# The experts' weights of a fused attention and mixture kernel: their transfers issued from GpSimd's queue instead of SyncE's

## The chip, the cores and the metric

The kernel runs on one core of one Trainium2 chip. The metric is the device time of one execution in microseconds (us); the median of three runs of the kernel before is 1012.65 us (1012.44 to 1013.64). In the rows PE is TensorE's matmul stream and PEld its weight loads, DVE is VectorE, ACT is ScalarE, POOL is GpSimd, SP is SyncE (SPq: instructions that SP's sequencer runs, here the issuing of DMAs).

## The reference

Three stages follow one another. First, attention inside chunks of 64 positions (8 batches, 8 heads, 576 positions, 64 numbers a head). Its output, 4608 tokens of 512 numbers, goes through a wide layer with a squared ReLU. Then comes a soft mixture of 8 experts with 4 slots each:

```python
x = attn(q, k, v)                                  # (4608, 512)
h = np.maximum(x @ w_in, 0.0)                      # w_in (512, 2048)
x = h * h @ w_out                                  # w_out (2048, 512)
logits = x @ phi                                   # phi (512, 32)
d = softmax(logits, axis=0)                        # over the tokens
slot_input = (d.T @ x).reshape(8, 4, 512)
for e in range(8):
    slot_out[e] = np.maximum(slot_input[e] @ w1[e], 0.0) @ w2[e]   # w1[e] (512, 1024), w2[e] (1024, 512)
out = softmax(logits, axis=1) @ slot_out           # (4608, 512), float32
```

No slot input is complete before the last token has gone through the wide layer, so the experts' matmuls stand at the end. Their weights, 32 MB in w1 and w2, are wanted only there.

## The kernel before

**Tiles and blocks.** The tokens are cut into 36 tiles of 128 (two chunks of 64 for all heads), and the tiles into 13 blocks of 1, 2 and then 3 tiles. For each of 16 slices f of the wide layer a step computes `hps = wi[f] x xb` (L764, 12 matmuls of 128x384), ReLU and square on ACT, a split into two halves of a number, `gh` (ACT, L178) and `gl` (DVE, L807), and adds `gh x wo[f]` and `gl x wo[f]` to the block's three output banks (L825, L826 with `gh`; L827 with `gl`). Numbers are carried as pairs of parts, so each product costs three matmuls. While PE works on block b, the other engines run the attention of the tiles of block b+1; POOL has four operations of it, the halves of v (L433), the normalised weights (L484) and their low part (L497). Two DMA transposes of a tile go through SP (L444, L500).

**After a block.** The generator `soft` turns a finished block into logits and running sums: `largest_of`, then for blocks 5 to 11 each tile's two parts are written to `x16` (ACT L1019, DVE L1020), transposed by a DMA from SP into `x2T` (L1024, three of them), and multiplied with phi (L1032, 36 matmuls for three tiles j = 0, 1, 2). The last block takes another way (L1044, L1056), and it is followed by the chain that joins the running maxima and sums, on whose way POOL has six operations: low parts of the transposed routing weights (`cT`, L1270) and copies for the next ones (`c`, L187), which PE transposes (L1256).

**The experts' weights.** `units` lists 64 pieces of 512 KB: 32 of w1 (128 rows of 1024 numbers, 4 KB in a row) and 32 of w2 (four runs of 256 numbers, 1 KB each, in a partition). There is no room for them during the kernel, so `load_units` puts a piece wherever a buffer has had its last reader: `give(...)` hands a buffer over, `load_units` takes the next piece of the list, and issues it whole or, where the two free halves do not lie side by side, in two halves of 256 KB. The first six go out in block 4 (`parts_of_wo` gives the second half of `wo`), most others when the attention's buffers of the last two tiles, 34 and 35, come free, and then one by one in the last block, as each `wi` and `wo` has been used for the last time. The rest follow in the experts' stage itself, with the output stores behind them.

**What sets the order.** Up to block 2 a list written by the kernel's own planner fixes every engine's order. From there on the Tile framework's scheduler orders each engine's queue by its own estimates, PE excepted after the end of the last block, where the program's order holds. Each queue is worked off in order: an instruction that waits holds up all behind it, a DMA's issue as well. All DMAs before were issued by SP: attention's loads (L377), w_in and w_out (L271), the transposes, the experts' pieces (L1194, L1197 for w1, L1203, L1208 for w2), the output.

Of the kernel before, what the change touches and what calls it, by code (L numbers as in the profile page):

```python
# [74 lines left out]
def kernel(  # L75
# [25 lines left out]
    dve, act, pool, pe, sp = nc.vector, nc.scalar, nc.gpsimd, nc.tensor, nc.sync  # L101
# [654 lines left out]
    def moe_h(b, f):  # L756
        n = blocks[b][1] * P
        xb = xb_b[max(group[b], 1) % 2][:, :, :, bank0.get(b, 0) * P :]
        bank = ps_h.tile([P, 512], F32, tag="h", name="hps")
        hp = bank[:, :n]  # L760
        nm = 0
        for kt in range(KT):
            for wl, xl in ((0, 0), (0, 1), (1, 0)):
                pe.matmul(  # L764
                    hp, wi[f][:, wl, kt], xb[:, xl, kt, :n], start=(nm == 0), stop=(nm == 3 * KT - 1)
                )
                nm += 1
        gt[b, f] = {"hp": hp, "n": n}
        while after_h:
            after_h.pop(0)(bank)  # L770
# [12 lines left out]
    def moe_relu(b, f, eng="act"):  # L783
        r = gt[b, f]
        r["g"] = half_of("g", F32)[:, : r["n"]]
        sc = (act_w if parts16(b) else inv_w)[:, f : f + 1]
        if eng == "act":
            act.activation(out=r["g"], in_=r["hp"], func=ACTF.Relu, scale=sc)  # L788
        else:
            dve.tensor_scalar(r["g"], r["hp"], sc, 0.0, ALU.mult, ALU.max)  # L790

    def moe_square(b, f, eng="act"):
        g = gt[b, f]["g"]
        if eng == "act":
            act.activation(out=g, in_=g, func=ACTF.Square)  # L795
        else:
            (dve if eng == "dve" else pool).tensor_tensor(out=g, in0=g, in1=g, op=ALU.mult)

    def moe_gh(b, f, eng="act"):
        r = gt[b, f]  # L800
        r["gh"] = half_of("gh", F16 if parts16(b) else F32R)[:, : r["n"]]
        copy(eng, r["gh"], r["g"])

    def moe_gl(b, f, eng="dve"):
        r = gt[b, f]
        r["gl"] = half_of("gl", F16 if parts16(b) else F32R)[:, : r["n"]]
        (dve if eng == "dve" else pool).tensor_tensor(  # L807
            out=r["gl"], in0=r["g"], in1=r["gh"] if parts16(b) else r["gh"].bitcast(F32),
            op=ALU.subtract,
        )  # L810
# [365 lines left out]
    home, free, size_of = {}, [], {}  # L1176
    todo = list(units)

    def load_units():
        while todo and len(free) > 1:  # L1180

            whole = [x for x in range(len(free) - 1) if free[x][0] is free[x + 1][0]]
            x = whole[0] if whole else 0
            a, b = free[x : x + 2]
            del free[x : x + 2]
            u = todo.pop(0)
            m, ch, e, kk = u
            whole_home = a[0] is b[0] and a[1] + 512 == b[1]
            places = [t[:, o : o + 512] for t, o, _ in (a, b)]
            home[u] = (a, b)  # L1190
            if m == 0:
                src = w1[e, kk * P : (kk + 1) * P, :]
                if whole_home:
                    sp.dma_start(out=a[0][:, a[1] : a[1] + 1024], in_=src)  # L1194
                else:
                    for h, pl in enumerate(places):
                        sp.dma_start(out=pl, in_=src[:, h * 512 : (h + 1) * 512])  # L1197
            else:
                src = w2[e, kk * RT * P : (kk + 1) * RT * P, ch * DH : (ch + 1) * DH].rearrange(
                    "(t p) d -> p t d", p=P  # L1200
                )
                if whole_home:
                    sp.dma_start(  # L1203
                        out=a[0][:, a[1] : a[1] + 1024].rearrange("p (t d) -> p t d", d=DH), in_=src
                    )
                else:
                    for h, pl in enumerate(places):
                        sp.dma_start(  # L1208
                            out=pl.rearrange("p (t d) -> p t d", d=DH), in_=src[:, h * RT // 2 : (h + 1) * RT // 2]
                        )  # L1210

# [74 lines left out]
    def run_gen(t, gen):  # L1286
        def go(t=t):
            try:
                next(gen)
            except StopIteration:  # L1290
                return
            at(t + 1, lambda: go(t + 1))
        at(t, lambda: go(t))
# [245 lines left out]
    def put_until(t):  # L1539
        while tokens and tokens[0][0] < t:  # L1540
            put(*tokens.pop(0)[2:])
# [4 lines left out]
    def give(*tags):  # L1546
        for pl, tag, n in tags:
            if tag in kept_tags[: (C_CHAIN + 1) // 2]:
                empty.update({(tag, 0), (tag, 512)})
            else:  # L1550
                freed(pl, tag, n)
        load_units()
# [8 lines left out]
    pl = (NT - 1) % 2  # L1561
# [12 lines left out]
    while t < end or any(x >= t for x in slots):  # L1574
        put_until(t + 1)
        b, f = steps[t] if 0 <= t < len(steps) else (None, None)
        if b is not None:
            moe_h(b, f)
            moe_relu(b, f)
            moe_square(b, f)  # L1580
            if (b, f) == (NB - 1, NF - 1):
                give((big, f"xb{b % 2}", 1536))
        for fn in slots.pop(t, []):
            fn()
        if b is not None:
            moe_gh(b, f)
            moe_gl(b, f)
            if b == NB - 1 and f % 2:
                give((big, f"wi{f // 2}", 1024))
        if 0 <= t - LAG < len(steps):  # L1590
            b, f = steps[t - LAG]
            moe_out(b, f, f == 0, f == NF - 1)
            if b == F16_FROM - 1:
                parts_of_wo(f)
            if b == NB - 1 and f == 0:
                give((big, "wo16", 512))
            elif b == NB - 1 and (f % 2 == 0 or f == NF - 1):
                give((big, f"wo{(f - 1) // 2}", 1024))
            if f == NF - 1:
                if b == NB - 1:  # L1600
                    if TAIL_ORDER:
                        ctx.enter_context(
                            tc.manual_schedule(
                                engines={getattr(mybir.EngineType, e) for e in TAIL_ORDER}
                            )
                        )
                    give(*[(big, x, 512) for x in ("g0", "g1", "gh", "gl")])
                moe_store(b, True)
                gen = soft(b)
                run_gen(t + 1 if b < NB - 1 else t, gen)  # L1610
                if b == NB - 1:
                    slots[t].pop()()
        t += 1
# [221 lines left out]
```

## Time and profile before

| | us |
|---|---|
| median of three runs | 1012.65 |
| profiled execution | 1012.46 |
| its span on the core | 1010.7 |
| PE busy | 942.7 |
| DVE busy | 659.5 |
| ACT busy | 545.1 |
| POOL busy | 263.6 |

The span is the time from the first to the last instruction; the profiled execution took 1.76 us more than its span. Busy times overlap. PE's idle time lies mostly in the first fifth and in the last tenth of the span; in between it has work nearly all the time, and the other engines wait for it or for one another.

The experts' pieces are 92 issues on SP in all, 36 of 512 KB and 56 of 256 KB.

### The profile page before, as it was taken

To read this page: it belongs to the slowest core of one execution; us is meant where nothing else is said; L and a number is where in the kernel's file an instruction comes from. 1 tells how busy PE (TensorE), PEld (TensorE's weight loads), DVE (VectorE), ACT (ScalarE), POOL (GpSimd) and SP (SyncE) were. 2 spreads that over 40 slices of the span, in tenths; PEclk is the share of its full clock that TensorE was granted. 3 is DMA by queue.
4 is the path that set the end of the run, shared out by engine and by line. 5 is a ranking of instruction groups with operands and counts; after the bars stand their busy time and mean duration, and the time that the engine had idled before them with its cause. 6 is when DMAs were issued, how large, how long until landed. Compare 5 with 4: busy or idle time off the path is not lost.

```text
span 1010.7 us, 18866 instructions
## 1 busy us (share of the span) xinstructions
PE 942.7 (93%) x7277; PEld 569.5 (56%) x7277; DVE 659.5 (65%) x1395; ACT 545.1 (54%) x1022; POOL 263.6 (26%) x265
## 2 busy tenths in 40 slices
PE   6778999899999999999999999999999999999892
PEld 5566666577666665555555555555555545555352
DVE  4998958656788877677677686586686742322242
ACT  4677664445567664455555564555555644544232
POOL 3587544423124441121112111111211110000200
PEclk9799999999999999999999999999999999999997
DMA  6767232325432463334354454353353651466898
GB/s 161 228 175 194 74 122 53 64 63 88 97 68 63 108 143 64 63 69 90 63 98 82 67 117 78 63 95 64 63 95 63 143 139 53 105 198 191 275 359 258
DMA packets 270762, 117.70 MB, mean 116 GB/s; under 512 B 230224, under 2 KB 264016, under 8 KB 270672
## 3 DMA queue, kind: packets, MB, share of 16 engines
q1 hardware_dynamic: 270672, 116.49, 48.1%
q8 instruction: 57, 0.93, 0.4%
q14 instruction: 33, 0.27, 0.1%
HBM read 78.71 MB, written 9.44 MB: 87 GB/s over the span
## 4 chain that ended last, share of the span: by engine, by line
PE 64%; DVE 17%; DMA 6%; ACT 3%; issue 3%; SPq 3%; POOL 2%; DVEq 0%; POOLq 0%; ACTq 0%
PE hps L764 25%; PE x L825 9%; PE x L827 9%; PE x L826 9%; DMA qkv<-in_k_dram 3%; DVE qk L293 2%; DVE stage L298 2%; PE ehps L1657 2%; PE sop L1773 2%; DVE gl L807 1%; SPq L377 1%; DVE qk L292 1%; PE misc L1147 1%; DMA qkT<-qk 1%; DMA x2T<-x 1%
## 5 line engine op out<-in xcount | busy, mean ns | idle before, releaser
L764 PE MATMUL hps<-xb,wi 128*128 128x384 f16 (+2 forms) x2412 | 411.3, 320 | 3.1 <-DVE wi L331 2.3
L764 PEld LDWEIGHTS <-wi 128*128 128x128 f16 x2412 | 224.5, 98 | 156.2 <-issue 14.3
L825 PE MATMUL x<-wo,gh 128*128 128x512 f16 (+1 forms) x576 | 229.4, 398 | 2.9 <-DVE x2sb L891 2.9
L826 PE MATMUL x<-wo,gh 128*128 128x512 f16 (+1 forms) x576 | 222.1, 386 | 0.0
L827 PE MATMUL x<-wo,gl 128*128 128x512 f16 (+1 forms) x576 | 206.6, 389 | 7.7 <-DVE gl L807 4.5
L807 DVE TENSOR_TENSOR gl<-g,gh 128x384 f16<-128x384 f32 (+1 forms) x162 | 94.8, 590 | 96.8 <-ACT gh L178 95.4
L788 ACT ACTIVATE g<-hps,act_w 128x384 f32<-128x384 f32 x128 | 73.9, 577 | 154.3 <-PE hps L764 136.7
L178 ACT ACTIVATE gh<-g 128x384 f16<-128x384 f32 (+3 forms) x196 | 99.8, 509 | 20.7 <-PE x L826 16.4
L484 POOL TENSOR_TENSOR ex<-ex,rs 128x512 f32<-128x512 f32 x29 | 31.2, 1077 | 287.0 <-DVE rs L481 127.2
L795 ACT ACTIVATE g<-g 128x384 f32<-128x384 f32 (+2 forms) x196 | 99.7, 509 | 5.1
L172 DVE TENSOR_REDUCE am<-qkv 128x1 bf16<-128x512 f32 x94 | 63.7, 685 | 47.5 <-DMA qkv<-in_k_dram 23.8
L433 POOL TENSOR_SCALAR vbd<-qkv,as 64x512 f16<-64x512 f32 x58 | 53.8, 927 | 155.9 <-DVE ai L208 144.9
L827 PEld LDWEIGHTS <-gl 128*128 128x128 f16 x384 | 37.1, 98 | 47.4 <-DVE gl L807 4.6
L825 PEld LDWEIGHTS <-gh 128*128 128x128 f16 x384 | 37.6, 98 | 42.6 <-ACT g L788 5.0
L788 ACT ACTIVATE g<-hps,inv_w 128x384 f32<-128x384 f32 (+1 forms) x72 | 38.6, 536 | 40.5 <-PE hps L764 26.3
L826 PEld LDWEIGHTS <-gh 128*128 128x128 f16 x384 | 37.6, 98 | 39.3 <-issue 4.0
L423 DVE SCALAR_TENSOR_TENSOR qk<-qkv,as,qk 128x512 f16<-128x512 f32 x58 | 55.0, 958 | 0.9 <-ACT qk L418 0.5
L448 DVE COPY qbd<-qkT 64x1024 f16<-64x1024 f16 x58 | 26.6, 459 | 44.2 <-DMA qkT<-qk 43.7
L438 DVE SCALAR_TENSOR_TENSOR vbd<-qkv,as,vbd 64x512 f16<-64x512 f32 x58 | 51.3, 884 | 3.8 <-POOL vbd L433 2.8
L807 POOL TENSOR_TENSOR gl<-g,gh 128x384 fp32r<-128x384 f32 (+2 forms) x39 | 43.1, 1108 | 36.8 <-ACT gh L178 28.4
L474 ACT ACTIVATE ex<-ex,es 128x512 f32<-128x512 f32 x29 | 20.8, 718 | 43.8 <-DVE ex L468 43.8
L827 PEld LDWEIGHTS x<-wo,gl 128*128 128x128 f32 x192 | 35.5, 189 | 15.5 <-POOL gl L807 5.2
(240 smaller groups left out, 1413.0 us busy)
## 6 DMA issues: line engine op xcount, KB each, us to landing
unit<-in_moe_w_dram SPq DMA_DIRECT2D x36, 512.0 KB, 4.3
unit<-in_moe_w_dram SPq DMA_DIRECT2D x56, 256.0 KB, 5.9
qkv<-in_q_dram SPq DMA_DIRECT2D x72, 128.0 KB, 3.2
qkv<-in_k_dram SPq DMA_DIRECT2D x72, 128.0 KB, 3.4
qkv<-in_v_dram SPq DMA_DIRECT2D x72, 128.0 KB, 3.3
stage<-in_moe_w_in_dram SPq DMA_DIRECT2D x16, 512.0 KB, 4.1
stage<-in_moe_w_out_dram SPq DMA_DIRECT2D x16, 512.0 KB, 5.5
out_dram<-o SPq DMA_DIRECT2D x14, 512.0 KB, 5.6
```

The costliest lines, as they stand in the source:

```text
L172: dve.tensor_reduce(out=am, in_=src, axis=AX.X, op=ALU.max, apply_absolute_value=True)
L178: act.activation(out=out, in_=in_, func=ACTF.Copy)
L423: dve.scalar_tensor_tensor(out=qk16[:, 2 * a + 1], in0=flat[:, a], scalar=v["s"][:, a : a + 1], in1=qk16[:, 2 * a], op0=ALU.mult, op1=ALU. ...
L433: pool.tensor_scalar(out=dst[0], in0=vin, scalar1=v["s"][pr, 2:3], scalar2=1.0, op0=ALU.mult, op1=ALU.mult,)
L438: dve.scalar_tensor_tensor(out=dst[1], in0=vin, scalar=v["s"][pr, 2:3], in1=dst[0], op0=ALU.mult, op1=ALU.subtract,)
L764: pe.matmul(hp, wi[f][:, wl, kt], xb[:, xl, kt, :n], start=(nm == 0), stop=(nm == 3 * KT - 1))
L788: act.activation(out=r["g"], in_=r["hp"], func=ACTF.Relu, scale=sc)
L795: act.activation(out=g, in_=g, func=ACTF.Square)
L807: (dve if eng == "dve" else pool).tensor_tensor(out=r["gl"], in0=r["g"], in1=r["gh"] if parts16(b) else r["gh"].bitcast(F32), op=ALU.subtract,
L825: pe.matmul(o, gh[:, c], w[:, 0], start=first, stop=False)
L826: pe.matmul(o, gh[:, c], w[:, 1], start=False, stop=False)
L827: pe.matmul(o, gl[:, c], w[:, 0], start=False, stop=last)
```

## The change

A list of one entry, `unit_queue`, holds the engine that issues the pieces. It starts as GpSimd and is set to SyncE when the last block's last step has been written out. So 42 of the 92 issues move from SP to POOL: the 28 whole and 8 half pieces that make up all of w1, and six whole pieces of w2. SP keeps two whole pieces and 48 halves of w2.

```diff
+    unit_queue = [pool]
+
     def load_units():
...
                 if whole_home:
-                    sp.dma_start(out=a[0][:, a[1] : a[1] + 1024], in_=src)
+                    unit_queue[0].dma_start(out=a[0][:, a[1] : a[1] + 1024], in_=src)
                 else:
                     for h, pl in enumerate(places):
-                        sp.dma_start(out=pl, in_=src[:, h * 512 : (h + 1) * 512])
+                        unit_queue[0].dma_start(out=pl, in_=src[:, h * 512 : (h + 1) * 512])
...
                 if whole_home:
-                    sp.dma_start(
+                    unit_queue[0].dma_start(
                         out=a[0][:, a[1] : a[1] + 1024].rearrange("p (t d) -> p t d", d=DH), in_=src
                     )
...
-                        sp.dma_start(
+                        unit_queue[0].dma_start(
                             out=pl.rearrange("p (t d) -> p t d", d=DH), in_=src[:, h * RT // 2 : (h + 1) * RT // 2]
                         )
...
             if f == NF - 1:
                 if b == NB - 1:
+                    unit_queue[0] = sp
```

Line numbers behind the change are two higher (three in the experts' stage): L1194 and L1197 become L1196 and L1199, L1203 and L1208 become L1205 and L1210, L1270 becomes L1272.

The scheduler answers with another order on other engines too. POOL, where the attention of tiles 34 and 35 ends (`qkv_77`, `ex_81`, `p_83` belong to tiles with odd numbers, `ex_80`, `p_82` to tile 34; `c_...` are copies of routing weights). Before:

```order
L497 TENSOR_TENSOR p_83<-ex_81,p_83 128x512
L433 TENSOR_SCALAR vbd<-qkv_77,as 64x8x64 x2
L484 TENSOR_TENSOR ex_80<-ex_80,rs 128x512
L497 TENSOR_TENSOR p_82<-ex_80,p_82 128x512
L187 TENSOR_SCALAR c_10219<-cmat 128x512
L484 TENSOR_TENSOR ex_81<-ex_81,rs 128x512
L497 TENSOR_TENSOR p_83<-ex_81,p_83 128x512
```

The same place of POOL's queue now:

```order
L497 TENSOR_TENSOR p_83<-ex_81,p_83 128x512
L1196 DMA unit<-in_moe_w_dram 128x1024
L1199 DMA unit<-in_moe_w_dram 128x512
L1196 DMA unit<-in_moe_w_dram 128x1024 x3
L433 TENSOR_SCALAR vbd<-qkv_77,as 64x8x64 x2
L1196 DMA unit<-in_moe_w_dram 128x1024
L1199 DMA unit<-in_moe_w_dram 128x512
L484 TENSOR_TENSOR ex_80<-ex_80,rs 128x512
L497 TENSOR_TENSOR p_82<-ex_80,p_82 128x512
L187 TENSOR_SCALAR c_10219<-cmat 128x512
L1199 DMA unit<-in_moe_w_dram 128x512
L1196 DMA unit<-in_moe_w_dram 128x1024
```

Five issues now stand ahead of tile 35's L433, two ahead of tile 34's L484, and four (of which two are shown) ahead of tile 35's L484.

POOL at the end of the last block, before:

```order
L908 MEMSET siT 128x1152
L1270 TENSOR_TENSOR cT<-c_10219,cT 64x512
L187 TENSOR_SCALAR c_10814<-cmat 128x512
L1270 TENSOR_TENSOR cT<-c_10254,cT 64x512
L187 TENSOR_SCALAR c_10819<-cmat 128x512
```

and now:

```order
L908 MEMSET siT 128x1152
L1196 DMA unit<-in_moe_w_dram 128x1024
L1199 DMA unit<-in_moe_w_dram 128x512
L1196 DMA unit<-in_moe_w_dram 128x1024 x8
L1199 DMA unit<-in_moe_w_dram 128x512
L1196 DMA unit<-in_moe_w_dram 128x1024 x5
L1205 DMA unit<-in_moe_w_dram 128x4x256 x6
L1272 TENSOR_TENSOR cT<-c_10219,cT 64x512
L187 TENSOR_SCALAR c_10814<-cmat 128x512
L1272 TENSOR_TENSOR cT<-c_10254,cT 64x512
L187 TENSOR_SCALAR c_10819<-cmat 128x512
```

All issues of the last block, the six pieces of w2 last, stand ahead of the first `cT` operation.

PE at the logits of block 10, in the first steps of block 11 (`x2T_9485` are the transposed tiles, `x_0`, `x_1`, `x_2` the output banks). Before, all 36 matmuls L1032 stand in a row; here is the last of them, and what follows:

```order
L1032 LDWEIGHTS x_4365
L1032 MATMUL misc<-x2T_9485,x_4365 32x128
L825 LDWEIGHTS gh
L825 MATMUL x_0_9401<-wo_3605,gh 128x512
L826 LDWEIGHTS gh
L826 MATMUL x_0_9401<-wo_3605,gh 128x512
L827 LDWEIGHTS gl
L827 MATMUL x_0_9401<-wo_3605,gl 128x512
```

Now, from the first of them:

```order
L1032 LDWEIGHTS x_4365
L1032 MATMUL misc<-x2T_9485,x_4365 32x128
L1032 LDWEIGHTS x_4365
L1032 MATMUL misc<-x2T_9485,x_4365 32x128
L825 LDWEIGHTS gh
L825 MATMUL x_0_9401<-wo_3605,gh 128x512
L826 LDWEIGHTS gh
L826 MATMUL x_0_9401<-wo_3605,gh 128x512
L825 LDWEIGHTS gh
L825 MATMUL x_1_9402<-wo_3605,gh 128x512
L826 LDWEIGHTS gh
L826 MATMUL x_1_9402<-wo_3605,gh 128x512
```

Two of the 36 come first, for tiles 0 and 1; then the six matmuls with `gh`, then the other 34, whose first is the first to read tile 2.

## Rows read from the trace of the kernel before

**Rows 1.** The page, part 1: busy time, share of the span, instructions.
```profile
PE 942.7 (93%) x7277; PEld 569.5 (56%) x7277; DVE 659.5 (65%) x1395; ACT 545.1 (54%) x1022; POOL 263.6 (26%) x265
```

**Rows 2.** Waits of PE, 330 to 870 us: total, times, longest (us).
```profile
PE x L827 <- DVE gl L807: 4.2, 6, 1.1
PE misc L1032 <- DMA x2T<-x: 2.4, 3, 1.2
```

**Rows 3.** PE in order of time, blocks 10 and 11: start, us, instruction, [idle before <-releaser].
```profile
740.72 0.85 PE L1032 MATMUL misc<-x2T,x 128*32 128x128 f16 x36
...
809.89 0.22 PE L1032 MATMUL misc<-x2T,x 128*32 128x128 f16 x1
811.33 0.22 PE L1032 MATMUL misc<-x2T,x 128*32 128x128 f16 x1 [1.23 <-DMA x2T<-x]
812.11 0.83 PE L1032 MATMUL misc<-x2T,x 128*32 128x128 f16 x34 [0.57 <-DMA x2T<-x]
812.88 0.61 PE L825 MATMUL x<-wo,gh 128*128 128x512 f16 x1
...
816.50 3.09 PE L764 MATMUL hps<-xb,wi 128*128 128x384 f16 x18
...
823.09 0.19 PE L511 MATMUL misc<-pT,vbd 128*128 128x64 f16 x1
```

**Rows 4.** The chain that ended last, one piece in block 11.
```profile
820.02 0.22 PE x L825
```

**Rows 5.** Busy time by stretch: window, length, PE, PEld, DVE, ACT, POOL, PEclk, DMA, GB/s.
```profile
814.00:815.00 1.00, 1.00 (x4) 0.32 (x3) 1.00 (x4) 0.66 (x3) 0.01 (x1) 0.50 0.89 123
```

**Rows 6.** SP's queue in order of time, blocks 10 and 11.
```profile
733.86 4.00 SPq L1024 DMA_TRANSPOSE x2T<-x  x3
...
801.95 0.81 SPq L1194 DMA_DIRECT2D unit<-in_moe_w_dram  x2
802.85 1.23 SPq L1024 DMA_TRANSPOSE x2T<-x  x1
804.17 2.97 SPq L1024 DMA_TRANSPOSE x2T<-x  x1
807.20 2.18 SPq L1024 DMA_TRANSPOSE x2T<-x  x1
809.78 2.88 SPq L444 DMA_TRANSPOSE qkT<-qk  x1
...
813.85 1.23 SPq L500 DMA_TRANSPOSE pT<-p  x1
...
827.83 0.37 SPq L1194 DMA_DIRECT2D unit<-in_moe_w_dram  x1
```

**Rows 7.** The pieces' issues: count, ns min/median/max of one, first and last start.
```profile
L1194 SPq DMA_DIRECT2D unit<-in_moe_w_dram x28: 327/328/1262, 345.3 to 913.9; - x28
```

**Rows 8.** POOL in order of time, block 4 and tiles 34 and 35.
```profile
356.50 1.04 POOL L484 TENSOR_TENSOR ex<-ex,rs 128x512 f32<-128x512 f32 x1 [1.98 <-DVE xi L234]
...
805.44 1.48 POOL L433 TENSOR_SCALAR vbd<-qkv,as 64x512 f16<-64x512 f32 x2 [17.67 <-DVE ai L208]
810.11 1.15 POOL L484 TENSOR_TENSOR ex<-ex,rs 128x512 f32<-128x512 f32 x1 [3.19 <-DVE rs L481]
...
831.33 1.04 POOL L484 TENSOR_TENSOR ex<-ex,rs 128x512 f32<-128x512 f32 x1 [17.32 <-DMA unit<-in_moe_w_dram]
```

**Rows 9.** SP's queue at the end of the last block, whole pieces of w2.
```profile
926.08 0.37 SPq L1203 DMA_DIRECT2D unit<-in_moe_w_dram  x1
...
929.98 0.37 SPq L1203 DMA_DIRECT2D unit<-in_moe_w_dram  x1
```

**Rows 10.** The chain that ended last, behind the last block.
```profile
935.44 1.27 POOL cT L1270
...
938.85 0.63 POOL c L187
939.52 0.66 PE cps L1256 x4
```

## The prediction

> **What bounds the kernel now.** I began with the page's first part: PE is busy for 942.7 of 1010.7 us [rows 1], so only what holds PE back can move the time, and a queue that is relieved gains nothing unless PE waited behind it. Next I read PE's waits over the blocks that follow the planner's part. They are short, the two longest groups 4.2 and 2.4 us [rows 2]. The first (L827 behind DVE) belongs to turns from one block to the next and knows nothing of DMAs. The second, L1032 behind the transposes of `x2T`, is one that SP's queue can cause. PE's order of time shows where it lies: at 809.89 PE begins the logits of block 10, waits 1.23 us for the second tile and 0.57 us for the third [rows 3]. One block earlier the same 36 matmuls ran in one piece, with no wait [rows 3]. Then I looked at the granted clock: behind that wait it is 0.50, that is 1.2 GHz in place of 2.4, for some microseconds, after PE had been nearly idle from 810 to 812 [rows 5]. The nine matmuls from 812.88 to 816.50 take 3.62 us [rows 3]; at the 0.22 us that one takes a few microseconds later [rows 4] they would take 1.98. So this place costs 0.57 + 1.23 + 1.64 = 3.4 us.
>
> Why the transposes were late is to be seen in SP's queue. Two pieces of 512 KB were issued at 801.95, and right behind them, at 802.85, the first transpose; the second held SP for 2.97 us and the third for 2.18, where three together took 4.00 a block earlier [rows 6]. Their data were in time: the first transpose left 0.9 us behind the pieces. What was in the way were the pieces, one megabyte in front of them in the same queue.
>
> **The change part by part.**
>
> *SP loses 42 issues.* One costs it 0.33 us, of w2 0.37 [rows 7, 9], and SP is on PE's path only at the place above. Without the pieces ahead in its queue, the three transposes should go as in block 10: there PE's logits ran without a wait 740.72 - 733.86 = 6.9 us behind the first issue [rows 3, 6]. 802.85 + 6.9 = 809.7, just before PE's 809.89. That would take away all of 1.80 us of waiting. The megabyte still moves at that time, from another queue, so I leave 0.4 us of waiting. The new order helps on its own: behind the logits' first two matmuls stand six matmuls with `gh`, 6 x 0.22 = 1.3 us of work, before the first that reads the third tile, so the wait of 0.57 is covered even if the transposes land as late as before. With PE no longer empty for two microseconds I count the clock's 1.64 us as regained. Bounds for this place: 0.57 us (only the order helps) and 3.4 us (all of it); I take 3.0, nearer to the upper one, because the row of block 10 shows what the transposes do without pieces ahead of them.
>
> *POOL gains 42 issues.* No row shows such an issue on POOL. From below it is what SP takes, 0.33 us [rows 7]. From above: POOL's own instruction on a tile is 1.27 us [rows 10], and if an issue went by runs, a piece of w2 with four runs in a partition would cost four times as much, 5.1 us. I take 1.27 us for either kind, since it is POOL's own row, and keep 0.33 and 5.1 for the range. POOL is 26% busy [rows 1], so the sum (42 x 1.27 = 53 us) matters only where something stands behind an issue:
>
> - Block 4, six issues between POOL's operations. POOL idled 1.98 us before its L484 there [rows 8], more than one issue. Cost nothing; at 5.1 us a few microseconds on attention work that PE doesn't wait for there.
> - Ahead of tile 35's L433 now stand the two pieces that SP issued at 801.95 [rows 6]: 801.95 + 2 x 1.27 = 804.5, and L433 started at 805.44 [rows 8]. Covered up to 1.7 us an issue.
> - Ahead of tile 34's L484 (810.11 [rows 8]) stand two issues that wait for DVE's and POOL's last readers of tile 35's inputs. The transpose of tile 35's q and k waits for the same DVE operations and left at 809.78 [rows 6], so I let both issues go then: 809.78 + 2 x 1.27 = 812.3. That makes this L484 2.2 us late, and the transpose L500, at 813.85 [rows 6], as well. Three transposes in a row were ready 6.9 us behind the first issue (above), so one is ready in no more; PE's L511 wants it at 823.09 [rows 3], 9.2 us behind 813.85. 9.2 - 6.9 = 2.3 us: covered, though at 5.1 us an issue it is not.
> - Ahead of tile 35's L484 (831.33 [rows 8]) stand four more, the last of which SP issued at 827.83 [rows 6], 3.5 us before. Covered at 1.27 us; and tile 35 is wanted only by the last block.
> - The end of the last block. The last four whole pieces of w2 are let go from 926.08 to 929.98 [rows 9], all ahead of POOL's first `cT`, which started at 935.44 and lies on the chain: `cT`, `c`, `cT`, `c`, then PE's L1256 at 939.52 [rows 10]. Each microsecond by which POOL is late here is one of the whole kernel. POOL is through at 929.98 + 1.27 = 931.3, or, with the four queued, at 926.08 + 4 x 1.27 = 931.2. That is 4.1 us before it is wanted. The cover is gone from (935.44 - 926.08) / 4 = 2.34 us an issue, and from there the kernel loses four times what is above it.
>
> *The transfers themselves.* The bytes are the same, and w1 is read only behind the last block. I cost it at nothing.
>
> *The other moves.* The scheduler shifted a handful of DVE, ACT and PE instructions in blocks 4, 10 and 11. I count them at nothing, with 1.5 us to either side: a turn between blocks waits up to 1.1 us at L827, and so much may come or go [rows 2].
>
> **The sum.** 1012.46 (the profiled execution, 1.76 us more than its span) - 3.0 = 1009.5. The median of the runs lies 0.2 us above that execution: 1009.7.
>
> **The rivals.**
>
> *The pieces are in the way from another queue as well.* The transposes then land as late as before: the wait of 1.23 stays, that of 0.57 is covered by the order, the clock comes back or not. Gain 0.57 to 2.2, middle 1.4: 1011.3. For it: the same megabyte leaves at the same time, and the third transpose took 2.18 us of SP's time although it was issued 5 us behind the pieces [rows 6]. Against it: the pieces would no longer stand in front but beside. The Trainium skill ("DMA: Bandwidth & Descriptors", section "Issuing engines are not separate DMA queues") speaks for this rival: DMAs of all issuers end on the same 16 engines and interleave there, and other issuers save only the time of issuing.
>
> *Slower: POOL's issues of w2 hold up the chain behind the last block.* It decides from 2.34 us an issue. At 4.0 us POOL is through at 926.08 + 16 = 942.1, 6.6 us late; with the gain of 3.0 the kernel ends 3.6 us later than now, at 1016.3. By the upper bound of 5.1 it is 11 us late. For it: four runs in a partition; no spare engine behind POOL there [rows 10]. Against it: POOL would have to take three times its own 1.27 us. The Trainium skill ("SBUF — State Buffer", section "SBUF: two separate sides") has a rule that speaks for it: GpSimd writes the descriptors of its DMAs into SBUF and is locked out while VectorE holds the port that they share, and a transfer of 620 ns became 3100. No run here shows that yet. By the figure 3.1, an estimate, POOL would be 4 x 3.1 - 9.36 = 3.0 us late, and the gain gone.
>
> *The new order gives back elsewhere what it saves.* Two turns of blocks more with a wait as in rows 2 (1.1 us), or POOL's lateness in tiles 34 and 35 passed on through DVE: 2.6 us, so 1012.3. For it: DVE and PE have their rows changed in blocks 4, 10 and 11, and such turns wait in some blocks and not in others. Against it: PE has work of its own beside each of the moved rows.
>
> **How the numbers follow.** Forecast 45%, pieces in the way 25%, POOL late 15%, given back 15%. Some 0.2% (2.0 us) is what a measurement of this kernel can tell from no change, so faster means below 1010.6 and slower above 1014.7. Faster: nearly all of the forecast (42), a part of the second case (6), a little of the fourth (2): 50%. Slower: most of POOL late (11) and a little of the fourth (2): 13%. The rest, 37%, within. The forecast's own range is 1008.2 to 1011.2. The whole range goes from 1008.0 up to 1014.5, which takes in the second and the fourth case, and POOL late up to about 3.5 us an issue (1012.65 - 3.0 + 4.6 = 1014.3); dearer issues than that are left out.
>
> **What would show it.** Right: no wait of PE, or one under half a microsecond, at block 10's logits, the granted clock 1.00 behind them, SP's three transposes in some 4 us; POOL's first `cT` still waiting for ACT, not for its own queue. Wrong: an issue on POOL over 2.3 us; L1256 waiting longer for POOL than now; a wait at L1032 as before; a new wait at L511 of tile 34.

## The result and the profile after

The changed kernel is slower, by 1.5%. Its median is 1027.73 us (1023.45 to 1032.79) beside 1013.14 us (1012.44 to 1014.27) for the kernel before on the same chip; the ratio is 1.0147, 95% interval 1.0115 to 1.0178. Forecast were 1009.7 us, 1014.5 at most. The profiled execution took 1032.79 us, the longest of the four, with a span of 1031.0; it shows the loss larger than the median does. Of all executions in this document one, of the kernel `e10` below, took 1938 us, nearly twice its like; it is left out of that kernel's median.

PE's waits between 330 and 935 us, as in [rows 2] (columns: total us, times, longest):

```profile
PE x L827 <- DVE gl L807: 12.2, 6, 6.7
PE misc L1032 <- DMA x2T<-x: 2.8, 4, 1.2
PE misc L1138 <- ACT dts L1092: 2.4, 1, 2.4
```

The wait at block 10's logits, which was to go, is still there (1.2 us is its longest). Two others are new, of 6.7 and 2.4 us. SP's issues between 793 and 831 us (start, us on SP), which answer to [rows 6]:

```profile
793.37 1.25 SPq L500 DMA_TRANSPOSE pT<-p  x1
794.74 2.11 SPq L444 DMA_TRANSPOSE qkT<-qk  x1
817.39 6.44 SPq L1024 DMA_TRANSPOSE x2T<-x  x3
824.43 3.16 SPq L444 DMA_TRANSPOSE qkT<-qk  x1
```

SP is free of pieces, as intended, and yet the three transposes of `x2T` hold it for 6.44 us; from the first one's start to the last one's end it was 6.53 us before. POOL's issues in that time:

```profile
794.98 0.61 POOL L1196 DMA_DIRECT2D unit<-in_moe_w_dram  x1 [1.63 <-DVE qk L423]
795.58 0.54 POOL L1199 DMA_DIRECT2D unit<-in_moe_w_dram  x1
817.50 1.05 POOL L1196 DMA_DIRECT2D unit<-in_moe_w_dram  x2 [6.71 <-PE misc L461]
824.91 0.58 POOL L1196 DMA_DIRECT2D unit<-in_moe_w_dram  x1 [3.39 <-issue]
825.49 0.54 POOL L1199 DMA_DIRECT2D unit<-in_moe_w_dram  x1
```

Each time pieces leave within 0.5 us of a transpose's issue. For tile 34 the profile names the reason: POOL waited for DVE's L423, which is the last to read the `qkv` buffer and also writes the `qk` that is transposed, so one operation lets both go. The chain of waits (start, us) shows what becomes of the two transposes, of tiles 34 and 35:

```profile
794.74 14.95 DMA qkT<-qk
824.43 11.35 DMA qkT<-qk
```

Before, these two landed in 5.3 and 4.3 us. The row of all 29 transposes L444 puts them beside their like (here before, then after):

```profile
DMA to landing us min/median/max: 4.3/4.6/6.3
```
```profile
DMA to landing us min/median/max: 4.3/4.6/14.9
```

DVE in order of time (start, us, and in brackets what it waited). First the copy L448 of tile 34 before, then the changed kernel:

```profile
794.47 0.86 DVE L448 COPY qbd<-qkT 64x1024 f16<-64x1024 f16 x2 [3.41 <-DMA qkT<-qk]
```
```profile
796.08 0.56 DVE L807 TENSOR_TENSOR gl<-g,gh 128x384 f16<-128x384 f32 x1 [0.94 <-ACT gh L178]
809.71 0.86 DVE L448 COPY qbd<-qkT 64x1024 f16<-64x1024 f16 x2 [13.07 <-DMA qkT<-qk]
810.60 0.56 DVE L807 TENSOR_TENSOR gl<-g,gh 128x384 f16<-128x384 f32 x1
```

The copy L448 of the attention waits 13.07 us in DVE's queue, and the next `gl`, which PE needs, stands behind it:

```profile
811.21 0.61 PE L827 MATMUL x<-wo,gl 128*128 128x512 f16 x1 [6.72 <-DVE gl L807]
```

The wait of 2.4 us has the same shape, with tile 35's transpose. Its copy L448 held up the running maximum of the logits (DVE L1088 and L1091), and through it ACT's L1092, for which PE waits:

```profile
835.80 0.86 DVE L448 COPY qbd<-qkT 64x1024 f16<-64x1024 f16 x2 [6.66 <-DMA qkT<-qk]
```
```profile
837.79 0.42 PE L1138 MATMUL misc<-ident,dts 96*128 96x96 f32 x1 [2.37 <-ACT dts L1092]
```

The engines around tile 34's wait, in stretches of 2 us (length; busy PE, PEld, DVE, ACT, POOL; granted clock, DMA share, GB/s):

```profile
804.00:806.00 2.00, 0.49 (x3) 0.00 (x0) 0.00 (x0) 0.00 (x0) 0.00 (x0) 1.00 1.28 83
806.00:808.00 2.00, 0.00 (x0) 0.00 (x0) 0.00 (x0) 0.00 (x0) 0.00 (x0) 0.69 1.12 98
808.00:810.00 2.00, 0.00 (x0) 0.00 (x0) 0.29 (x1) 0.00 (x0) 0.00 (x0) 0.50 0.16 52
812.00:814.00 2.00, 2.00 (x6) 0.63 (x5) 2.00 (x4) 0.39 (x1) 0.00 (x0) 0.50 0.56 213
814.00:816.00 2.00, 2.00 (x35) 1.72 (x33) 0.82 (x5) 1.30 (x3) 0.00 (x0) 0.50 0.00 0
816.00:818.00 2.00, 2.00 (x29) 1.53 (x27) 1.99 (x4) 1.17 (x2) 0.50 (x1) 0.75 0.00 0
```

From 806 to 808 us PE, DVE, ACT and POOL all stand still, the granted clock falls to 0.50 (1.2 GHz) and stays there after PE has work again. The DMA share stays at 1.12 to 1.28 up to 808 us, while only 83 to 98 GB/s move: the 16 DMA engines are busy, but few bytes pass.

POOL's issues themselves are cheap (line, times | busy us, mean ns | idle before), and the first `cT` behind the last block still waits for other engines:

```profile
L1196 POOL DMA_DIRECT2D unit<-in_moe_w_dram x28 | 15.4, 551 | 86.3 <-PE hps L764 25.6 <-PE misc L513 17.1 <-DMA qkT<-qk 14.1
L1205 POOL DMA_DIRECT2D unit<-in_moe_w_dram x6 | 4.5, 754 | 11.8 <-PE hps L764 7.5 <-PE x L827 3.1 <-ACT x2sb L180 1.2
L1272 POOL TENSOR_TENSOR cT<-c,cT 64x512 fp32r<-64x512 f32 x4 | 5.0, 1267 | 6.4 <-PE mps L931 4.4 <-ACT c L1271 1.9
```

Where the span grew: the stage from `x2T` of block 9 to that of block 10 (first issues on SP, 733.86 to 802.85 before, 739.33 to 817.39 after) by 9.1 us, the next one by 4.4, the last block by 1.1. Of the remaining 5.7 us, 3.2 lie ahead of 230 us, where no instruction was moved, so they are scatter of this execution (kernels of this layout reach that point between 228.6 and 233.2 us).

### The profile page after: what moved, and what is told of

The parts are those of the page before. It is cut to its first block, busy times and chain, and to the rows that moved or that the text cites. A ratio compares the mean times of both kernels' runs of the same rounds, so it can differ in the third digit from the quotient of the medians.

```text
span 1031.0 us, 18885 instructions
## 1 busy us (share of the span) xinstructions
PE 951.0 (92%) x7277; PEld 572.8 (56%) x7277; DVE 660.3 (64%) x1395; ACT 545.0 (53%) x1022; POOL 282.8 (27%) x307
## 4 chain that ended last, share of the span: by engine, by line
PE 62%; DVE 17%; DMA 9%; issue 4%; ACT 4%; POOL 2%; SPq 2%; DVEq 0%; POOLq 0%; ACTq 0%
PE hps L764 25%; PE x L825 9%; PE x L827 9%; PE x L826 8%; DMA qkT<-qk 4%; DVE gl L807 2%; DMA qkv<-in_k_dram 2%; PE ehps L1660 2%; DVE qk L293 1%; PE sop L1776 1%; DMA qkv<-in_q_dram 1%; DVE stage L298 1%; DMA x2T<-x 1%; DVE vbd L438 1%; DVE qk L292 1%
## 5 line engine op out<-in xcount | busy, mean ns | idle before, releaser
L827 PE MATMUL x<-wo,gl 128*128 128x512 f16 (+1 forms) x576 | 207.6, 392 | 15.7 <-DVE gl L807 12.5
L484 POOL TENSOR_TENSOR ex<-ex,rs 128x512 f32<-128x512 f32 x29 | 31.5, 1087 | 270.3 <-DVE rs L481 134.4
L433 POOL TENSOR_SCALAR vbd<-qkv,as 64x512 f16<-64x512 f32 x58 | 50.9, 877 | 140.7 <-DVE ai L208 129.4
L827 PEld LDWEIGHTS <-gl 128*128 128x128 f16 x384 | 37.3, 99 | 56.6 <-DVE gl L807 13.7
L448 DVE COPY qbd<-qkT 64x1024 f16<-64x1024 f16 x58 | 26.4, 455 | 58.5 <-DMA qkT<-qk 58.0
L438 DVE SCALAR_TENSOR_TENSOR vbd<-qkv,as,vbd 64x512 f16<-64x512 f32 x58 | 54.2, 934 | 2.2 <-POOL vbd L433 1.1
L423 DVE SCALAR_TENSOR_TENSOR qk<-qkv,as,qk 128x512 f16<-128x512 f32 x58 | 52.8, 920 | 0.9 <-ACT qk L418 0.5
L827 PEld LDWEIGHTS x<-wo,gl 128*128 128x128 f32 x192 | 35.7, 190 | 16.2 <-POOL gl L807 5.4
```

What stands on the lines that cost most here:

```text
L423: dve.scalar_tensor_tensor(out=qk16[:, 2 * a + 1], in0=flat[:, a], scalar=v["s"][:, a : a + 1], in1=qk16[:, 2 * a], op0=ALU.mult, op1=ALU. ...
L433: pool.tensor_scalar(out=dst[0], in0=vin, scalar1=v["s"][pr, 2:3], scalar2=1.0, op0=ALU.mult, op1=ALU.mult,)
L438: dve.scalar_tensor_tensor(out=dst[1], in0=vin, scalar=v["s"][pr, 2:3], in1=dst[0], op0=ALU.mult, op1=ALU.subtract,)
L827: pe.matmul(o, gl[:, c], w[:, 0], start=False, stop=last)
```

## The experiments

Theory A: a transpose on SP's queue is stretched by copies that POOL's queue runs beside it. B: POOL's load and order do it, anywhere. C: any second queue does it. D: it takes the work of the other engines.

**Parts of the change.** Four kernels on one chip (before: 1011.86 us median). `e1` issues the pieces for the buffers of tiles 34 and 35 from SP again, `e2` only these from POOL:

```diff
     def after_attention(pr, more=()):
+        unit_queue[0] = sp       # e2: pool
         give(...)
+        unit_queue[0] = pool     # e2: sp, as everywhere else
```

> Only the pieces that go into the attention buffers of tiles 34 and 35 are issued from SP again; block 4 and the last block stay on POOL. Theory A (a DMA transpose is stretched by a copy that POOL's queue runs beside it; in the changed kernel the qkT transposes of tiles 34 and 35 took 14.9 and 11.4 us to land in place of 4.6): both land within 6.5 us again, PE has no empty stretch of microseconds between 780 and 850, and of the 14.6 us between the medians some 12 are gone: 1015 us (1012 to 1017.5), what is left being block 4. Rival B (it is POOL's load and the scheduler's order, in any place): the loss is spread, over 1020 us.

> The opposite: only the pieces that go into the attention buffers of tiles 34 and 35 are issued from POOL, all others from SP. Theory A (transposes stretched by POOL's copies beside them): nearly all of the loss, 1025 us (1021 to 1029), a qkT landing of 11 us or more at tile 34 or 35. Rival B (spread over all POOL issues): a third of it or less, under 1018 us.

`e5` starts with SP and turns to POOL at the last block's first step; `e6` turns to POOL around `parts_of_wo` alone.

> Only the pieces issued one by one in the last block go from POOL, all earlier ones from SP. Theory A: there are no attention transposes there, only the three x2T of block 11, which PE doesn't wait for; as before, 1012.7 us (1011 to 1014.5), and POOL's issues again cost 0.53 us (w1) and 0.75 us (w2) without reaching the chain behind the last block. Rival (POOL's issues hold its cT operations): over 1015 us.

> Only the six pieces of block 4 go from POOL, all others from SP. The profile of the changed kernel lay 4.2 us behind before these six and 6.6 us behind it, two attention tiles later. Theory A: the transposes of those two tiles run partly beside the copies; a loss of 1 to 4 us, 1015 us (1012.5 to 1017). Rival (the six pieces cost nothing, and the early lag is scatter of one execution): 1012.7 us.

| pieces from POOL | median us | ratio to before, 95% |
|---|---|---|
| all but tiles 34, 35 (e1) | 1014.49 | 1.0022 (1.0008 to 1.0037) |
| tiles 34, 35 only (e2) | 1017.07 | 1.0056 (1.0035 to 1.0077) |
| last block only (e5) | 1013.57 | 1.0018 (0.9997 to 1.0040) |
| block 4 only (e6) | 1012.59 | 1.0006 (0.9991 to 1.0021) |

e1 came out as A had it: 1014.49 us, and no `qkT` took over 6.0 us. e2 did not: 1017.07 us is 5.2 over before, not the 1025 expected, and under the 1018 that stood for B. So these parts alone do not decide between A and B. The chain of e2 shows what was smaller than A had taken:

```profile
790.61 10.26 DMA qkT<-qk
814.62 8.89 DMA qkT<-qk
```

Here the transposes took 10.26 and 8.89 us in place of 14.95 and 11.35; DVE's `gl` then held PE for 2.1 us, not 6.7. In another execution of the changed kernel (`c1` below) they landed in 8.13 and 8.9 us, and PE waited 0.77 for tile 34's `gl`. So the stretch varies from one execution to the next. The landing of tile 34's transpose is covered up to some 8 us, and beyond that it is paid in full, in the profile above with the clock on top. e5 and e6 are not told apart from before; A's estimate for block 4 (1015 us) was missed. The parts add up to some 8 us, the whole change costs 12 to 15; that difference is not settled.

**The transfers by themselves.** A kernel with only transposes and copies; DVE touches the sources to let a group go and reads each target to see it land.

> The transfers by themselves: no attention, no layer, no experts; six repeats each of a transpose of 128x2048 (as qkT) or 128x1024 (as pT) and of copies of 512 or 256 KB, alone and together, on SP's, POOL's and ACT's queues. The output is not computed. Theory A (POOL's software queue is special): transpose alone 4 to 5 us to landing, a copy alone 3 to 4.5 us from any queue, transpose and copy one behind the other on SP 6 to 8 us in all, transpose beside a POOL copy 10 to 15 us for both, beside an ACT copy under 8 us. Theory C (any second queue): beside an ACT copy 10 to 15 us as well. Theory D (only DVE, POOL or memory traffic of the full kernel makes it slow): beside a POOL copy under 8 us here too.

DVE's reads (start, us; in brackets the wait for the landing). A 128x2048 transpose alone; with a 512 KB copy ahead of it on SP; beside one from POOL; beside one from ACT; beside 512 KB of w2 from POOL:

```profile
9.74 0.16 DVE L79 SCALAR_TENSOR_TENSOR seen<-qkT,seen 128x1 f32<-128x1 f16 x1 [4.50 <-DMA qkT<-qk]
...
153.36 0.16 DVE L79 SCALAR_TENSOR_TENSOR seen<-qkT,seen 128x1 f32<-128x1 f16 x1 [1.70 <-DMA qkT<-qk]
...
194.87 0.16 DVE L79 SCALAR_TENSOR_TENSOR seen<-qkT,seen 128x1 f32<-128x1 f16 x1 [9.26 <-DMA qkT<-qk]
195.07 0.16 DVE L79 SCALAR_TENSOR_TENSOR seen<-unit,seen 128x1 f32<-128x1 f32 x1
...
254.22 0.16 DVE L79 SCALAR_TENSOR_TENSOR seen<-qkT,seen 128x1 f32<-128x1 f16 x1 [5.89 <-DMA qkT<-qk]
...
417.97 0.16 DVE L79 SCALAR_TENSOR_TENSOR seen<-qkT,seen 128x1 f32<-128x1 f16 x1 [6.61 <-DMA qkT<-qk]
```

Counted from DVE's first touch of the group to the read (six repeats): alone 4.6 us; behind a copy on SP 6.0 to 6.6; beside POOL's copy 9.5 to 11.0; beside ACT's 6.1 to 6.2; beside w2 from POOL 6.9 to 7.0. A copy alone takes 3.6 us from SP, 4.0 to 4.7 from POOL. So a transpose and a copy that take 4.6 + 4.3 us one by one take 10 together. One behind the other on SP they take 6.0 to 6.7 us in all. The rows of the pair with POOL's copy show that both are stretched (median us from issue to landing of six):

```profile
unit<-in_moe_w_dram POOLq DMA_DIRECT2D x6, 512.0 KB, 8.7
qkT<-qk SPq DMA_TRANSPOSE x6, 9.6
```

POOL's issue stands 0.3 us behind SP's, so they end within some 0.6 us of one another. The Trainium skill ("DMA: Bandwidth & Descriptors", section "Queues, rings and completion order") has each DMA engine take turns between its queues, a packet of one and then of the other; that both end together agrees. Why POOL's copy doubles the time of both is not told by that: beside ACT's queue the copy landed in 3.9 us and the transpose in 5.8. So for the transfers by themselves no load of DVE or POOL is needed, and ACT's queue doesn't do it: there A holds, and C and D do not.

The same with the kernel's own groups, and with other lengths of run:

> The transfers by themselves once more (no attention, no layer, no experts; the output is not computed), six repeats each, in the kernels' own groups: a transpose of 128x1024 (pT) and one of 128x2048 (qkT) on SP, and 512 + 256 KB of w1 behind them on SP, or from POOL, or from ACT; three transposes of 128x1024 (x2T) with two pieces of 512 KB ahead of them or behind them on SP, or from POOL; and one transpose of 128x2048 beside 512 KB from POOL in runs of 2 KB, 1 KB and 512 bytes. Theory A: from POOL the qkT lands at 12 to 15 us, behind on SP at 5 to 6, from ACT at 7 to 10 (10.1 in the kernel that used ACT); the stretch falls with the length of a run (about 10 us at 4 KB, 7 at 1 KB in the first measurement). Rival (it needs the other engines' work): from POOL under 10 us, no difference by runs.

| group (us from its release to landing, typical of six) | pT or x2T | qkT or last x2T |
|---|---|---|
| pT, qkT, then 512 + 256 KB on SP | 3.8 | 6.2 |
| the same, pieces from POOL | 6.1 | 9.4 |
| the same, pieces from ACT | 6.3 | 7.9 |
| x2T x3 alone | 3.9 | 6.5 |
| two pieces ahead on SP, x2T x3 | 6.8 | 8.8 |
| x2T x3, two pieces from POOL | 6.2 | 10.4 |
| x2T x3, two pieces behind on SP | 3.9 | 6.5 |

This is the disputed place in small: three transposes behind two pieces on SP land 2.3 us late, beside POOL's pieces 3.9, and ahead of them on SP they lose nothing. The expected 12 to 15 us for qkT did not come: 9.4 us is under the 10 that stood for the other engines' work. What takes it to 15 in the full kernel stays open, and their work may have a part in that. 512 KB from POOL in two runs of 2 KB, four of 1 KB and eight of 512 bytes a partition gave 6.7 to 7.3, 6.8 to 7.1 and 7.2 to 7.5 us, one run of 4 KB some 10, but 256 KB in one run of 2 KB 8.1 to 9.4: a single run for a partition is worst, also at half the bytes (the copies in several runs read w2, the others w1).

**Another queue in the full kernel.** As e1, with `act` for `sp`.

> As the changed kernel, but the pieces that go into the attention buffers of tiles 34 and 35 are issued from ACT's hardware queue in place of POOL's software queue. Theory A: qkT of both tiles lands within 6.5 us; 1013 to 1019 us, the upper part if ACT, which works in order, is held by the buffers that it waits for. Theory C (any second queue beside a transpose): 10 to 15 us for a qkT that has a copy beside it, and 1022 us or more.

1024.95 us, ratio 1.0104 (1.0062 to 1.0146). A missed; both numbers, the time and tile 34's qkT of 10.14 us, are those that stood for C. That is more than alone beside ACT (6.2, or 7.9 in the kernel's group), so ACT's queue does little to the transfers by themselves, but not in the kernel; why was not followed up. Part of the loss is ACT's own: a piece for the buffer that the transpose reads has to wait for its landing, and ACT's next `g` stands behind that issue. PE waited 3.9 us for it.

```profile
802.85 0.58 ACT L788 ACTIVATE g<-hps,act_w 128x384 f32<-128x384 f32 x1 [8.03 <-DMA qkT<-qk]
```

PE's longest wait at L1032, 3.6 us, came in the last block, where POOL issues the pieces as in the changed kernel. As a way out ACT's queue is no better here.

**Holding the pieces back.** As the changed kernel, but a piece for tile 34's or 35's buffers can't leave before that tile's `qkT` has landed:

```diff
         def qdiag(c):
+            if i >= NT - 2 and c == 0:      # landed[..]: a tile of one number a partition
+                pool.tensor_copy(landed[i % 2], qkT_b[par][:, 0, :1])
...
+            if hold:                        # in load_units, before the DMA
+                for pl in places if not whole_home else places[:1]:
+                    pool.tensor_copy(pl[:, :1], hold[0])
```

> As the changed kernel, POOL's queue and the same bytes, but each piece for the attention buffers of tiles 34 and 35 is held back until that tile's qkT transpose has landed: POOL copies one column of qkT into a flag, and the flag into the first column of the piece's place, before the DMA writes it. Theory A (overlap is the cause): qkT lands within 6.5 us, PE's empty stretch behind it goes, 1015 us (1012 to 1019); the pieces may still meet x2T or pT transposes, which sets the upper end. Rival B (POOL's queue itself, its order and its waits): 1024 us or more, since POOL has the same issues and some 30 small operations more.

1005.92 us, 0.9923 (0.9895 to 0.9950): not 1015 but 8 us below *before*. The transposes of tiles 34 and 35 landed in some 4.6 us again:

```profile
qkT<-qk SPq DMA_TRANSPOSE x3, 4.6
```

(that row is of its repetition `c2`, 755 to 880 us; in `e10` below, the same tiles without the hold, it reads 9.3). But a part of its gain lay ahead of block 4 (a transpose L444 that the changed kernel issued at 318.4 us left at 311.7), where none of its instructions stands elsewhere. So controls were needed, four kernels on one chip: the changed kernel (`c1`), the held one (`c2`), and the changed kernel and the one before with the two flags written and never used (`e10`, `e12`).

> The changed kernel once more, on the chip of the next three, for a fair comparison: 1023 to 1033 us, a qkT landing of 10 us or more at tiles 34 and 35.

> The kernel that holds POOL's pieces for tiles 34 and 35 back until that tile's qkT has landed, once more, on another chip; it took 1005.9 us, 8 us less than the kernel before, though the loss to be regained was 14.6 us against the changed kernel only. If the hold is what makes it fast: 1004 to 1009 us again. If some of it was that chip: nearer to 1012.

> The control for the held kernel: the changed kernel with the two flags (POOL copies one column of qkT of tiles 34 and 35 into a small tile that is there in the held kernel too), but no piece waits for them. All engines' instructions stand in the same order as in the changed kernel, and the tiles lie where they lie in the held one. Theory A (holding the copies off the transposes is what helps): as the changed kernel, 1023 to 1033 us. Rival E (the small tile moves other tiles' addresses, and that is what helps): under 1015 us.

> The same control for the kernel before: its pieces on SP, plus the two flags on POOL and the small tile. No instruction of it stands elsewhere. If the addresses are what made the held kernel 8 us faster than before: some 6 to 8 us faster than before as well, 1005 us. If not: as before, 1011 to 1014 us.

| kernel | without flag tiles | with two flag tiles |
|---|---|---|
| pieces on SP | 1011.39 (before) | 998.76 (e12), 0.9866 (0.9839 to 0.9893) |
| pieces on POOL | 1023.13 (c1), 1.0108 (1.0082 to 1.0133) | 1011.30 (e10), 0.9991 (0.9965 to 1.0018) |
| on POOL, held | | 1003.27 (c2), 0.9910 (0.9884 to 0.9936) |

Two effects, and they add. The flag tiles alone give 11.8 to 12.6 us, whatever issues the pieces (theory E; what lies behind it is told below). The change costs 11.7 us without them and 12.5 with. And in the same layout, with the same queues and bytes, holding the pieces off the transposes gives back 8.0 of the 12.5 us; the intervals of e10 and c2 don't meet. The stages of the profiled executions, one of each kernel, show where (us; from the first issue of one block's `x2T` to the next block's, and from block 11's to POOL's first `cT`):

| kernel | start to block 9 | 9 to 10 | 10 to 11 | 11 to `cT` |
|---|---|---|---|---|
| before | 733.9 | 69.0 | 72.6 | 60.0 |
| after | 739.3 | 78.1 | 77.0 | 61.0 |
| c1 | 738.4 | 70.6 | 72.7 | 61.3 |
| e12 | 720.9 | 69.1 | 71.0 | 60.0 |
| e10 | 723.5 | 74.9 | 71.3 | 64.7 |
| c2 | 723.8 | 69.0 | 71.1 | 60.9 |
| e8 (below) | 735.1 | 68.9 | 69.1 | 60.0 |
| e16 (below) | 721.8 | 68.9 | 69.7 | 60.0 |

The hold takes the stage of tile 34's transpose from 74.9 us back to 69.0, the length that it has with the pieces on SP: that this stage's loss is overlap is shown. The last block is shorter too, by 3.8 us, though both kernels issue its pieces at the same distance from block 11's `x2T`; that part is scatter of the landings and not the hold's. Of the 4.5 us that are left between c2 and e12, 0.9 lie in the last block, where pieces still meet block 11's `x2T`, and 2.9 ahead of block 9. In the layout without flag tiles the account is less complete: of the 9.7 us by which c1's span is over before, only 3.1 lie in the three stages and 4.5 ahead of block 9, where kernels of that layout scatter from 733 to 739. In e10 the pieces met block 11's `x2T` harder:

```profile
872.32 10.08 DMA x2T<-x
```
```profile
882.45 0.83 PE L1036 MATMUL misc<-x2T,x 128*32 128x128 f16 x34 [2.70 <-DMA x2T<-x]
```

(its chain, and PE's wait for it). Block 4 was tried in the fast layout as well:

> The control with the two flags, with only block 4's six pieces issued from POOL. In the traces block 4 took 2.6 to 2.9 us more when POOL issued them, in this layout. If that is the cost: 1001.5 us (1000.5 to 1003). If it was scatter: 998.8 us.

1000.60 us (0.9877; 0.9851 to 0.9903). That is near the 1001.5 expected, but a control on that chip with its pieces on SP took 1001.53 (`e13`), so the medians show no cost. The traces of this layout do: from the last `qkT` issued ahead of block 4's pieces to block 5's `x2T`, 107.8 to 109.3 us in the four kernels that issue them from SP (e12, c3, e13, e16), 109.5 to 112.9 in the four that issue them from POOL (e15, e10, c2, e4). Whether block 4 has a part in the loss isn't settled.

**Where the tiles lie.** `e13` is the kernel before with two unused tiles of one number a partition.

> The kernel before with two small tiles of one number a partition, cleared once by POOL at its start and not used again; nothing else. Theory F (where the tiles lie is what made the control with the two flags 12.6 us faster than before): 997 to 1002 us. Rival (the two flag copies on POOL did it): as before, 1009 to 1014 us.

1001.53 us, 0.9886 (0.9857 to 0.9915): theory F holds; a part of the flags' copies in it is not to be seen (e12 0.9866).

**The place that the forecast spoke of.** The kernel before with its pieces on SP, those for tile 34 held until block 10's `x2T` has landed; `e8` has one flag tile, `e14` three, `e16` two, `c3` is e12 again, beside e16.

> The kernel before, with all pieces on SP, but the pieces for tile 34's attention buffers held back until block 10's x2T transposes have landed (a flag copied by POOL from x2T into the first column of each place). If the wait at block 10's logits comes from the two pieces in front of the transposes, as the prediction said, PE waits under 0.5 us there, the clock stays at 1.00, and 2 to 3.4 us are gained on the kernel before: 1009.9 us (1008.8 to 1011.5). If it doesn't come from them: within 1 us of the kernel before, or slower if POOL's held copies delay tile 35.

> The kernel before, in the layout with small flag tiles, its pieces on SP, with the pieces for tile 34's buffers held until block 10's x2T has landed. The prediction's first step (the wait of 1.80 us and the clock's 1.64 at block 10's logits come from the pieces in front of the transposes): 2 to 3.4 us less than the control with the two flags, 996 us (995 to 998). If that place is worth nothing: 998.8 us.

> The kernel before with two small tiles in all (the layout that was 12 us faster), its pieces on SP, with the pieces for tile 34's buffers held until block 10's x2T has landed; one of the two tiles is the flag. Theory F (two such tiles make the layout fast, three do not: the kernel with three was 1014.4 us) and the place at block 10's logits worth some 2 us in this layout: faster than the control beside it by 1 to 2.5 us, 998 us on a chip where the kernel before takes 1012 to 1014. If the place is worth nothing: no difference. If the layout is not what counts: over 1008 us.

> The control of the kernel before with the two flags, once more, beside the last kernel: 998 to 1002 us.

e8: 1013.65 us, 0.9992 (0.9973 to 1.0012), and e14: 1014.38 us, 1.0004 (0.9986 to 1.0022): both missed. With one and with three tiles the layout is slow, and neither has a control with the same tiles, so their medians don't weigh the place. Their stages do: from block 10's `x2T` to block 11's they take 69.1 and 69.6 us, the kernels without the hold and with these pieces on SP 70.4 to 72.6 (before, e1, e5, e6). In e8 PE's longest wait for `x2T` there is 0.2 us. e16: 996.94 us (995.91 to 998.24), 0.9839 (0.9813 to 0.9865), beside c3's 999.24 (998.02 to 999.73), 0.9863. PE's waits between 760 and 870 us, e16 and then c3:

```profile
PE misc L513 <- DMA pT<-p: 0.7, 1, 0.7
```
```profile
PE misc L1036 <- DMA x2T<-x: 1.3, 2, 0.7
PE misc L1036 <- DVE xg L229: 0.7, 1, 0.7
```

Both waits for `x2T` are gone. By the medians this is worth 2.3 us, with four executions of each and ranges that touch; by the stage 1.3 us (71.0 in c3, 69.7 in e16). e16 is the fastest kernel of the study, 1.6% below before.

## Why the prediction was wrong

*The step that failed* is the one on the transfers themselves: "The bytes are the same, and w1 is read only behind the last block. I cost it at nothing." It asked who waits for the copies, not who runs beside them. The transposes of tiles 34 and 35 and of blocks 10 and 11 do: those of the tiles landed in 8.1 to 15.0 us in place of 5.3 and 4.3, those of block 11's `x2T` that PE waited for in 8.1 (after) and 10.1 us (e10), where before no wait for them appears. Instead of nothing it cost the larger part of the loss: the hold regains 8.0 of 12.5 us by the medians, and 5.9 us in tile 34's stage of the profiled pair. The same error is in the first step, which took a piece that is no longer in front of a transpose to be out of its way and left 0.4 us of waiting; 1.21 us stayed. And the reading of [rows 2], that PE's waits at L827 know nothing of DMAs, hid the path: DVE's copy of a transposed tile stands in the same queue ahead of the `gl` that L827 needs, and the longest new wait came there.

*The first step's place was real.* Pieces ahead of `x2T` on SP delay PE at block 10's logits; without them the waits go, and some 1 to 3.5 us are gained (e16, e8 and e14 by their stages; forecast 3.0, bounds 0.57 to 3.4). The new order did its part as forecast: the wait of 0.57 us is gone in the changed kernel, and the granted clock behind the logits is 1.00. But POOL's queue does not take the pieces out of the way: 10.4 us beside, 8.8 behind, 6.5 alone.

*POOL's issues* cost 0.55 and 0.75 us, in the range (0.33 to 5.1), under the value taken (1.27). None of the 42 took over 0.77 us. The cover at the tail held: POOL was through with its issues 4.4 us ahead of the first `cT` (forecast 4.1), which waits for PE. So the rival that is slower through POOL's issues at the tail is refuted. Slower had been given 13%, most of it for that reason, which was not the one.

*The rival "in the way from another queue"* named the right mechanism with the wrong sign. At block 10's logits it had it right: the wait of 1.23 us stays, that of 0.57 is covered. But it bounded the damage by what it was before, "the transposes then land as late as before". The Trainium skill's rule behind it ("DMA: Bandwidth & Descriptors", section "Issuing engines are not separate DMA queues") agrees in that the other issuer gained nothing but issue time; that it can cost is seen here only.

*The unmoved cover.* Tile 34's transpose (789 us before) was not on the list of steps, because no instruction of it moved. What changed was its neighbour: the piece that SP issued 2.1 us behind it now leaves 0.24 us behind it. DVE's and PE's cover there held for 8 us (0.77 us of wait at 8.13) and was gone at 15.

*The other moves*, and the rival that the new order gives the gain back: not separated. The held kernel has moves of its own in the same places and regains 8.0 of 12.5 us, so what is theirs lies within the other 4.5 or thereabouts.

## What to carry to other kernels

Moving a copy to another queue takes away its place in the order, which may have been what kept it off a transpose; ask of each transfer that is let go earlier what will run beside it, and keep the copies behind the transposes on one queue, or hold them by a real dependency. Before a difference of a per cent is explained, run the control that has the experiment's extra tiles and nothing else.

## What the runs showed that was not expected

**The place of the tiles is worth 12 us.** Each small tile takes 32 bytes of a partition in the built program and moves all attention and layer tiles behind it: the first `qkv` begins at byte 25,024 before, at 25,056 with one tile, 25,088 with two and 25,120 with three. Only 25,088 is a multiple of 128, and only there the kernel is fast (e12, e13, e15, e16, c2, e10 against their like); with 0, 1 and 3 tiles it is not (before, e8, e14). That e8 and e14 also hold pieces has no part in this, for the difference is there ahead of them: the eight profiled kernels with two tiles issue block 9's `x2T` at 721 to 727 us, the ten with none, one or three at 733 to 739. It is the DMAs that get faster. One stretch, 600 to 720 us, of before and then of e12 (packets, MB, share of 16 engines; issue to landing):

```profile
q1 hardware_dynamic: 36175, 9.03, 40.0%
...
qkT<-qk SPq DMA_TRANSPOSE x6, 4.5
```
```profile
q1 hardware_dynamic: 34688, 8.65, 34.1%
...
qkT<-qk SPq DMA_TRANSPOSE x5, 3.8
```

The share of e8 there is 40.3%, of e14 41.4%. The engines' time falls by a seventh for 4% fewer bytes, and DVE's wait for `qkT` over the kernel from 43.7 to 31.2 us. Which of the tiles matters, and whether 128 is the boundary or a larger power of two, was not tried.

**A wait that empties PE costs more than itself.** PE had next to no work from 804.5 to 811.2 us; its granted clock was 0.50 from 808 to 816 us and 0.75 in the two behind. At 0.50 the matmuls from 812 to 814 us followed one another every 0.43 us, in place of 0.22 ahead of the wait. The stage with the wait of 6.7 us grew by 9.1.
